# Three edits ahead of a matmul-bound stage: which queue issues loads, where weight roundings are doubled, and when weight sums begin

## The chip, the cores and the metric

The kernel runs on one core of a Trainium2 chip. The metric is the device time of one execution in microseconds, the median of three executions. PE is TensorE, DVE is VectorE, ACT is ScalarE, POOL is GpSimd and SP is SyncE. SP computes nothing here; it only issues DMAs. Every engine works through its own instructions in order.

## What is computed

Two blocks follow each other. The first is an attention with a threshold, for 8 batches of 8 heads, 576 rows and 64 values per head:

```python
scores = scale * np.matmul(q, k.transpose(0, 1, 3, 2))
thresh = np.max(scores, axis=-1, keepdims=True) - tau
scores = np.where(scores >= thresh, scores, -1000000000.0)
attn = np.exp(scores - max); attn = attn / (sum + 1e-09)
attn_out = np.matmul(attn, v)
```

(The last three lines are shortened.) The heads are put side by side, which gives `x`, 4608 rows of 512 values, and the second block follows:

```python
h = x @ w_in
r = np.maximum(h, 0.0)
g = r * r
return (g @ w_out).astype(np.float32)
```

`w_in` is 512 x 2048 and `w_out` is 2048 x 512, all in float32.

## The kernel before

**Steps.** Attention is cut into visits and steps. A visit `n` is a pair of heads of a batch (in the first batch, visits 0 to 3 take blocks 0 and 1 of it and visits 4 to 7 the rest); a step `s` is one block `i` of 128 query rows of a visit, for both heads. Block 4 is the leftover of 64 rows; the leftovers of the two heads, or from visit 12 on of two visits, share one step. There are 148 steps, and the main loop (L758 to L849) writes out the order of the work by hand, step after step. The trace has no step numbers; one counts the bursts of score matmuls on PE (L250), each of which starts a step.

**One step.** `scores` (L241) runs the score matmuls into PSUM and takes the row maxima on DVE (L272). `exponents` (L282) makes a bias and a threshold from the maxima and the exponents of both heads on ACT (L285, L286, L288). `threshold` (L291) applies the mask on DVE, one instruction per head (L300), and computes the reciprocals of the sums. `divide` (L305) scales the rows on POOL (L308, L310). A score tile of PSUM is free for the next step when its mask is done.

**Turning the weights of attention.** Up to visit 10, two steps later, PE transposes the rows (`turn`, L325) and ACT copies them to `wT`; three steps later `mix` (L433) multiplies with `v` (L436), and ACT puts the result into `xT`. From visit 11 on (`by_dma`, L602; its first step is 35, named `first_dma`), DVE transposes 32 x 32 squares (`turn_blocks`, L351, instruction L374) and SP places them with DMAs (`place_blocks`, L377, lines L386 to L399, 16 per call); visit 11's three placings come in steps 38, 39 and 40, and its `mix` in step 43.

**Loads.** `load_qk` (L160) issues the `q` and `k` rows of a visit on SP, except that for a `by_dma` visit it appends them with `load_part` (L177) to the list `loads`. `some_loads` (L191) is called four times a step; each call takes one or two entries from the front of that list and issues them on POOL (L194). Visit 11 is the one `by_dma` visit that goes through `load_qk` (step 31), and its `v` rows (`load_v`, L199, called at the end of step 34) go out on POOL too (L213). Later visits append directly, by the lists made at L708 to L741: in step 36 the `k` rows of visit 12, in step 37 those of visit 13 and the `q` rows of visit 12. `prep_part` (L227) transposes loaded rows on DVE (L230) into `qT` and `kT`. At the last step of a visit before `by_dma` (there `lay` is true, L786), `prep` does so for the next visit between the maxima and the masks. In the second step of such a visit, `split_left` (L220) copies the leftover query rows to `qmid` on ACT (L225).

**Roundings.** The weights arrive in 32 pieces, by DMAs on SP (L125), into three areas. Each piece is put into another form in five stages (`round_weights`, L127): two ACT instructions (stage 0, L138 and L139), one on DVE (stage 1, L141), one on DVE (stage 2, L143), two on POOL (stage 3, L145, and stage 4, L147). When it is done (`end_rounding`, L701), the area's next load is issued. The list `pieces` (L689 to L696) says how many pieces each step rounds. In a step with one, stage 1 stands between the exponents and the masks, stages 2 and 3 after the masks (in a `lay` step stage 1 too is after the masks). A second piece of a step (L824) has stages 1 to 3 after the masks. Steps with two are 16, 19 and 24, each of them a leftover step.

**Filling PE.** The matmuls of the second block are cut into filling pieces of eight matmuls (in the count of the trace): `mlp_in` (L477, matmuls L484), for the first chunk of 256 rows `mlp_out` (L511, L520), and for later chunks `product` (L539, L553). `fill` (L676) is called four times a step and puts pieces between the work of attention as far as the budget of the step allows (`rate`, L651) and as far as the weights they need were rounded by the step before last (`usable`). So a piece of weights that is rounded in an earlier step lets filling pieces move to an earlier step. The ACT and POOL work on their results is posted after the next piece.

**Weight sums.** The products of later chunks need sums of quarters of `w_out`, made by `some_sums` (L504) in 16 parts, one DVE instruction each (L508). They write where the areas of the arriving weights were (the first six parts) and beyond. A part is posted after each `mlp_in` piece of chunk 1 once `state["free"]` is set (L812), from the middle of step 36 on; `product` asks for those that it needs.

Of the kernel before, what the change touches and what calls it, by code (L numbers as in the profile page):

```python
# [19 lines left out]
def kernel(  # L20
# [10 lines left out]
    nc = tc.nc  # L31
# [4 lines left out]
    HP = H // 2  # L36
    NPAIR = B * HP
    NBLK = S // P
    REST = S - NBLK * P
# [66 lines left out]
    n_pieces = n_in + NFT * d_model // WP  # L106
# [43 lines left out]
    def rows_of(n):  # L150
        return rows_in[n % 2 if n <= 2 * HP else 0]
# [3 lines left out]
    def rows_32(t, n, m):  # L155

        b, h = divmod(visits[n][0], HP)
        return t[b, 2 * h + m // 2, :, (m % 2) * 32:(m % 2) * 32 + 32].rearrange("(c p) d -> p c d", p=32)

    def load_qk(n):  # L160


        if by_dma(n):
            load_part(k, n)
            load_part(q, n)
            return
        for x, t in ((rows_of(n)[1], k), (rows_of(n)[0], q)):
            for m in range(4):
                src, to = rows_32(t, n, m), x[m * 32:(m + 1) * 32, :, :]
                queue = nc.scalar if n == 0 and m % 2 else nc.sync  # L170
                last = REST // 32 if t is k and m >= 2 else 0
                queue.dma_start(out=to[:, last:, :], in_=src[:, 0:S // 32 - last, :])
                if last:
                    queue = nc.gpsimd if n == 0 else nc.sync
                    queue.dma_start(out=to[:, 0:last, :], in_=src[:, S // 32 - last:, :])

    def load_part(t, n):  # L177
        x = rows_of(n)[0 if t is q else 1]
        loads.extend((x[m * 32:(m + 1) * 32, :, :], rows_32(t, n, m)) for m in range(4))
# [11 lines left out]
    def some_loads():  # L191
        for _ in range(min(1 + (len(loads) > 8), len(loads))):
            to, src = loads.popleft()
            nc.gpsimd.dma_start(out=to, in_=src)  # L194

    def arrived(t):
        assert all(x[0].tensor.name != t.tensor.name for x in loads)
# [1 line left out]
    def load_v(n):  # L199
        b, h = divmod(visits[n][0], HP)  # L200
        h *= 2
        t = vs[n % 2]
        todo = []
        for u in range(2):
            at = u * (NBLK + 1)
            todo.append((t[:, at:at + NBLK, :], v[b, h + u, 0:NBLK * P, :].rearrange("(c p) d -> p c d", p=P)))
            for half in range(2):
                todo.append((t[half * D:(half + 1) * D, at + NBLK, :], v[b, h + u, NBLK * P:S, :]))
        if paired(n):
            loads.extend(todo)  # L210
            return
        for to, src in todo:
            (nc.gpsimd if by_dma(n) else nc.sync).dma_start(out=to, in_=src)  # L213

    def prep(n):

# [260 lines left out]
    def mlp_in(j, x):  # L477

        f, at = FORDER[x], j * TCH % RING
        if x % 2 == 0:  # L480
            used["h"] = take("mm", (6, 7)) if j < PLAIN else next_bank()
        h = used["h"].rearrange("p (f n) -> p f n", f=2)
        for c in range(NMC):
            nc.tensor.matmul(h[:, x % 2, :], w_in_sb[:, c, f * P:(f + 1) * P], xT[:, c, at:at + TCH],  # L484
                             start=(c == 0), stop=(c == NMC - 1))
        if x == NFT - 1:
            read_to["x"] = (j + 1) * TCH
        posts = []
        if j == PLAIN and state["free"]:
            posts.append(lambda: some_sums(1))  # L490
        if x % 2:
            def square():
                to = g[:, f - 1:f + 1, :]
                nc.scalar.activation(out=to, in_=h, func=AF.Relu)  # L494
                nc.gpsimd.tensor_tensor(out=to, in0=to, in1=to, op=ALU.mult)  # L495
                if j >= PLAIN and x % 8 == 7:
                    square_half(x // 8 * (HF // 2))
            posts.append(square)
        return posts

    sums = [(to, a, b, part) for to, a, b in ((FT1, Q01, Q00), (FT2, Q11, FT1), (FT4, FT2, Q10), (FT3, Q11, Q01))
            for part in range(4)]

    def some_sums(count):  # L504

        for to, a, b, part in sums[:count]:
            f = slice(part * 2, part * 2 + 2)
            nc.vector.tensor_tensor(out=wo[:, to, f, :], in0=wo[:, a, f, :], in1=wo[:, b, f, :], op=ALU.subtract)  # L508
        del sums[:count]
# [77 lines left out]
    FIRST = TCH // P  # L587
# [3 lines left out]
    def paired(n):  # L591

        return n >= 3 * HP
# [6 lines left out]
    PLAIN = 1  # L600

    def by_dma(n):  # L602

        return n >= 3 * HP - 1

    first_dma = next(s for s in range(NST) if by_dma(steps[s][0]))
# [19 lines left out]
    chunk_at, j = {}, 0  # L626
# [7 lines left out]
    state = {"us": 0.0, "left": 0.0, "step": 0, "free": False, "rounded": 0, "usable": 0, "then": [], "last": []}  # L634
# [55 lines left out]
    for s, (n, i) in enumerate(steps):  # L690
        if s < HP * FIRST:
            x = int(n > 0 and i == 0)
        else:
            x = 2 if HP + 2 <= n <= 2 * HP and i == NBLK else 1
        pieces.append(min(x, left))
        left -= pieces[-1]  # L696
    assert left == 0
# [58 lines left out]
    done = 0  # L756
    rounded_by = [0]
    for s in range(END + 1):  # L758
        state["step"] = s
        state["usable"] = rounded_by[-1]  # L760
        if s == 2:
            startup.close()
            bpsum = ctx.enter_context(tc.tile_pool(name="bpsum", bufs=1, space=bass.MemoryType.PSUM))
            bank.update((x, bpsum.tile([P, 512], FP32, tag=f"bank{x}", name=f"bank{x}")) for x in range(4, 8))
        rounded_by.append(state["rounded"])
        on = s < NST
        now = []
        if on:
            n, i = steps[s]
            at = visits[n][1].index(i)  # L770
            last = at == len(visits[n][1]) - 1
            now = list(range(done, done + pieces[s]))
            done += pieces[s]
            more = n + 1 < len(visits)
            short = n < 2 * HP
            if short and at == 0 and 0 < n + 1 < 2 * HP:
                load_qk(n + 2)
            elif not short and at == 1 and not by_dma(n):
                load_qk(n + 1)
            if now:  # L780
                round_weights(now[0], 0)
            if s != 1:
                scores(s)
        old = steps[s - 2] if 2 <= s < NST + 2 and not by_dma(steps[s - 2][0]) else None
        at_once = now or old or early()
        lay = on and last and more and not by_dma(n)  # L786
        if old:
            turn(*old, 0)
            turn(*old, 1)
        if on:  # L790
            exponents(n, i)
            for p in now[1:]:
                round_weights(p, 0)
            if at == 1:
                split_left(n)
            if lay:
                prep(n + 1)
            elif now:
                round_weights(now[0], 1)
        if s in mixes and not old:  # L800
            mix(*mixes[s])
            for j in chunk_at.get(s, ()):
                add_chunk(j)
        quarter = rate(s) / 4 if s < END else 1e9
        fill(quarter)
        if s in mixes and old:
            mix(*mixes[s])
            for j in chunk_at.get(s, ()):
                add_chunk(j)
        if old:  # L810
            turn(*old, 2)
        state["free"] = s > first_dma  # L812
        if s == 0:
            scores(1)
        if on:
            threshold(n, i)
            for fn in prep_at[s] + load_at[s]:
                fn()
            if lay and now:
                round_weights(now[0], 1)  # L820
            if now:
                round_weights(now[0], 2)
                round_weights(now[0], 3)
            for p in now[1:]:  # L824
                for stage in range(1, 4):
                    round_weights(p, stage)
            if not at_once:
                divide(n, i)
        if 0 < s <= NST and by_dma(steps[s - 1][0]):
            m, x = steps[s - 1]  # L830
            turn_blocks(m, x)
        for what in place_at[s]:
            place_blocks(*what)
        some_loads()
        fill(quarter)
        some_loads()
        if on and at_once:
            divide(n, i)
        fill(quarter)
        some_loads()  # L840
        fill(quarter)
        some_loads()
        if on:
            for p in now:
                end_rounding(p)
            if at == 0 and 0 < n <= 2 * HP:
                load_v(n)
            elif last and n >= 2 * HP and not by_dma(n):
                load_v(n + 1)  # L849
# [35 lines left out]
```

## Time and profile before

| | before |
|---|---|
| executions | 1394.46, 1396.89, 1398.92 us |
| profiled execution | 1396.9 us, span of the instructions 1395.1 us |
| PE, DVE, ACT, POOL busy | 97%, 60%, 31%, 65% of the span |
| PE busy in 0-100, 100-200, 200-300 us | 83.25, 94.79, 91.09 us |
| PE busy in 300-400 us | 100.00 us |
| granted PE clock, mean | 0.993 |
| SP DMAs that place (L386 to L399) | 1008 |

Busy time is the time in which an engine runs at least one instruction; issuing and waiting are not counted, except that the loads issued by POOL show up as POOL instructions (L194, L213). A row of a list of groups or of the timeline gives engine, line, operation, what is written from what (tile names without numbers), and a count; in square brackets stands the idle time before it and what ended it. `w`, and `wo` where L300 or L310 write it, are the tiles of attention rows: one of the three slots lies in the memory of `wo`. `turned` is scratch for roundings and, later, for the squares that are placed.

### The profile page before, as it was taken

Reading aid. Unit: us, or ns where it says so; the run is one execution under the profiler, and the core shown is the slowest. Engines: PE = TensorE matmul, PEld = TensorE weight load, DVE = VectorE, ACT = ScalarE, POOL = GpSimd, SP = SyncE. Lnnn points to the kernel's source line nnn. Section 1 sums busy time; section 2 is a strip of 40 time slices with the busy share of each in tenths; the row PEclk is TensorE's granted clock in tenths of the full one; section 3 lists DMA queues with packets and bytes.
Section 4 is the critical chain, followed back from the end, with each engine's and each line's share of the span. In section 5 each row is a group of like instructions: output and inputs, shape, how many; then the busy total and the mean of one; then the engine's idle time right before and its main releaser. Section 6 shows DMA issues by size and latency. Waiting matters only on the chain.

```text
span 1395.1 us, 22691 instructions
## 1 busy us (share of the span) xinstructions
PE 1356.8 (97%) x7576; PEld 1042.1 (75%) x7576; DVE 830.8 (60%) x1866; ACT 439.5 (31%) x1068; POOL 909.7 (65%) x1233
## 2 busy tenths in 40 slices
PE   6898998999999999999999999999999999999998
PEld 5676556777777778777777778777777877788887
DVE  5877774976767676757575666566666665401001
ACT  4776673223232323232323222222222222210110
POOL 3688877678696868676767677685867655422332
PEclk8999999999999999999999999999999999999999
DMA  8764521435646555554445455544444544310000
GB/s 153 156 146 135 135 64 40 78 80 110 118 95 110 112 104 116 99 115 85 98 84 115 82 111 109 109 79 101 90 99 89 121 87 101 63 35 16 0 16 16
DMA packets 397892, 127.95 MB, mean 92 GB/s; under 512 B 380336, under 2 KB 386576, under 8 KB 397776
## 3 DMA queue, kind: packets, MB, share of 16 engines
q1 hardware_dynamic: 374496, 93.07, 35.4%
q0 software_dynamic: 20976, 33.14, 8.9%
q8 instruction: 61, 1.00, 0.3%
q10 hardware_dynamic: 2304, 0.29, 0.2%
q14 instruction: 55, 0.45, 0.1%
HBM read 50.59 MB, written 9.44 MB: 43 GB/s over the span
## 4 chain that ended last, share of the span: by engine, by line
PE 89%; DVE 4%; ACT 2%; issue 2%; POOL 2%; DMA 1%; POOLq 0%; DVEq 0%; SPq 0%; ACTq 0%
PE bank L484 35%; PE bank L553 28%; PE s L250 12%; PE bank L436 10%; PE bank L520 2%; PE bank L334 2%; DVE wo L508 1%; DVE w L300 1%; ACT w L288 1%; DVE st L272 1%; ACT wT L335 1%; POOL kl L194 0%; POOL w L310 0%; DVE turned L374 0%; DVE wo L300 0%
## 5 line engine op out<-in xcount | busy, mean ns | idle before, releaser
L484 PE MATMUL bank<-xT,w_in_sb 128*128 128x256 f32 x2304 | 520.8, 383 | 1.1 <-ACT osb L526 1.1
L484 PEld LDWEIGHTS bank<-xT,w_in_sb 128*128 128x128 f32 x2304 | 432.2, 190 | 82.9 <-issue 22.2
L272 DVE TENSOR_REDUCE st<-s 128x1 f32<-128x576 f32 x286 | 203.9, 752 | 231.2 <-PE s L250 231.2
L300 DVE SCALAR_TENSOR_TENSOR w<-s,st,w 128x576 f32<-128x576 f32 x269 | 209.2, 814 | 119.4 <-ACT w L288 119.1
L553 PE MATMUL bank<-wo,gsum 128*128 128x256 f32 x1088 | 248.9, 382 | 2.1 <-POOL gsum L474 2.0
L310 POOL TENSOR_SCALAR w<-w,st 128x576 f32<-128x576 f32 x269 | 220.5, 829 | 25.2 <-DVE st L303 19.3
L553 PEld LDWEIGHTS bank<-wo,gsum 128*128 128x128 f32 x1088 | 204.0, 190 | 41.2 <-issue 9.8
L495 POOL TENSOR_TENSOR g<-g 128x512 f32<-128x512 f32 x144 | 151.3, 1051 | 97.6 <-ACT g L494 96.2
L285 ACT ACTIVATE st<-st 128x2 f32<-128x2 f32 (+1 forms) x148 | 30.3, 205 | 571.4 <-DVE st L272 570.6
L553 PE MATMUL bank<-wo,g 128*128 128x256 f32 x816 | 188.3, 382 | 0.0
L250 PE MATMUL s<-kT,qT 64*128 64x288 f32 x1016 | 168.2, 435 | 19.4 <-DVE w L300 6.9
L288 ACT ACTIVATE w<-s,st 128x576 f32<-128x576 f32 x269 | 183.1, 731 | 0.2 <-ACT st L286 0.2
L374 DVE STREAM_TRANSPOSE turned<-w 128x512 f32<-128x512 f32 (+2 forms) x388 | 168.8, 489 | 18.1 <-DMA wT<-turned 16.3
L308 POOL TENSOR_SCALAR st<-st 128x2 f32<-128x2 f32 (+1 forms) x148 | 33.4, 225 | 221.9 <-DVE w L300 214.7
L553 PEld LDWEIGHTS bank<-wo,g 128*128 128x128 f32 x816 | 153.0, 190 | 30.0 <-issue 8.3
L436 PE MATMUL bank<-wT,vs 128*64 128x128 f32 (+7 forms) x1700 | 167.9, 356 | 3.9 <-ACT wT L335 3.5
L436 PEld LDWEIGHTS bank<-wT,vs 128*64 128x64 f32 (+1 forms) x1700 | 95.7, 136 | 77.0 <-issue 23.8
L250 PEld LDWEIGHTS s<-kT,qT 64*128 64x128 f32 x1016 | 95.4, 189 | 76.6 <-issue 56.5
L494 ACT ACTIVATE g<-bank 128x512 f32<-128x512 f32 x144 | 86.0, 599 | 196.0 <-PE bank L484 195.3
L194 POOL DMA_DIRECT2D vs<-in_v_dram x144 | 90.5, 634 | 0.0
L567 DVE TENSOR_TENSOR gsum<-g 128x512 f32<-128x512 f32 x34 | 23.2, 714 | 110.6 <-PE bank L553 110.6
L194 POOL DMA_DIRECT2D kl<-in_k_dram x100 | 68.6, 689 | 0.0
(81 smaller groups left out, 997.4 us busy)
## 6 DMA issues: line engine op xcount, KB each, us to landing
wT<-turned SPq DMA_DIRECT2D x800, 72.0 KB, 2.3
out_dram<-osb POOLq DMA_DIRECT2D x34, 256.0 KB, 2.7
wo<-in_moe_w_in_dram SPq DMA_DIRECT2D x16, 512.0 KB, 4.7
wo<-in_moe_w_out_dram SPq DMA_DIRECT2D x16, 512.0 KB, 3.6
kl<-in_k_dram POOLq DMA_DIRECT2D x100, 72.0 KB, 3.0
ql<-in_q_dram POOLq DMA_DIRECT2D x100, 72.0 KB, 2.7
wT<-turned SPq DMA_DIRECT2D x192, 36.0 KB, 2.4
vs<-in_v_dram POOLq DMA_DIRECT2D x50, 128.0 KB, 3.2
```

The lines of the kernel that those rows point to most:

```text
L194: nc.gpsimd.dma_start(out=to, in_=src)
L250: nc.tensor.matmul(sc[u][to, half, 0:HALF], lhsT, keys[rows, half * HALF:(half + 1) * HALF], start=True, stop=True)
L272: nc.vector.tensor_reduce(out=mx[:, u:u + 1], in_=sc[u][:, :, 0:HALF], axis=AX.XY, op=ALU.max)
L288: nc.scalar.activation(out=w[:, u, :].rearrange("p (h k) -> p h k", h=2), in_=sc[u][:, :, 0:HALF], func=AF.Exp, bias=bias[:, u:u + 1], sca ...
L300: nc.vector.scalar_tensor_tensor(out=wu, in0=sc[u][:, :, 0:HALF], scalar=thr[:, u:u + 1], in1=wu, op0=ALU.is_ge, op1=ALU.mult, accum_out=s ...
L310: nc.gpsimd.tensor_scalar(out=w[:, u, :], in0=w[:, u, :], scalar1=z[:, u:u + 1], scalar2=rcp[:, u:u + 1], op0=ALU.add, op1=ALU.mult)
L374: nc.vector.transpose(wb[:, at:at + k1 - k0, i % 2, :], w[:, u, k0 * 32:k1 * 32].rearrange("p (k q) -> p k q", q=32))
L436: nc.tensor.matmul(ps[u * D:(u + 1) * D, :], vs[n % 2][rows, u * (NBLK + 1) + c, :], wT[rows, NBLK if c == NBLK else u * (NBLK + 1) + c, a ...
L484: nc.tensor.matmul(h[:, x % 2, :], w_in_sb[:, c, f * P:(f + 1) * P], xT[:, c, at:at + TCH], start=(c == 0), stop=(c == NMC - 1))
L494: nc.scalar.activation(out=to, in_=h, func=AF.Relu)
L495: nc.gpsimd.tensor_tensor(out=to, in0=to, in1=to, op=ALU.mult)
L553: nc.tensor.matmul(to, left[:, f, :], wo[:, slot, f, :], start=(f == 0), stop=(f == HF - 1))
```

## The change

There are three edits.

- Loads: `load_qk` no longer appends the loads of a `by_dma` visit to the list, but issues them at once on SP; `load_v` issues on SP where it issued on POOL; `some_loads` issues on SP up to step 37 and on POOL after that. This touches the eight `q` and `k` loads of visit 11, its six `v` loads, and the eight `k` loads of steps 36 and 37.
- Roundings: the steps with two pieces are 15, 18 and 22 instead of 16, 19 and 24. In such a step stage 1 of both pieces stands ahead of the masks; stages 2 and 3 of both follow after them. The order of the filling pieces on PE follows from what is `usable`: steps 15 to 28 hold 1,1,2,1,1,2,1,2,1,2,1,1,2,1 of them, where they held 1,1,0,2,2,0,3,1,1,2,1,2,1,2.
- Sums: the first parts may be made before `state["free"]`, up to six of them, as soon as all weight pieces are rounded. Parts per step, from 35 on: 2,4,4,3,3,0 where they were 0,2,4,3,5,2.

```diff
@@ load_qk
-        if by_dma(n):
-            load_part(k, n)
-            load_part(q, n)
-            return
         for x, t in ((rows_of(n)[1], k), (rows_of(n)[0], q)):
...
-                last = REST // 32 if t is k and m >= 2 else 0
+                last = REST // 32 if t is k and m >= 2 and not by_dma(n) else 0
@@ some_loads
-            nc.gpsimd.dma_start(out=to, in_=src)
+            (nc.gpsimd if state["step"] > first_dma + 2 else nc.sync).dma_start(out=to, in_=src)
@@ load_v
-            (nc.gpsimd if by_dma(n) else nc.sync).dma_start(out=to, in_=src)
+            nc.sync.dma_start(out=to, in_=src)
@@ mlp_in
-        if j == PLAIN and state["free"]:
+        if j == PLAIN:
             posts.append(lambda: some_sums(1))
@@ some_sums
+        done = 16 - len(sums)
+        count = min(count, (16 if state["free"] else 6 if state["rounded"] == n_pieces else 0) - done)
         for to, a, b, part in sums[:count]:
@@ pieces
-            x = 2 if HP + 2 <= n <= 2 * HP and i == NBLK else 1
+            x = 2 if (n, i) in ((2 * HP - 2, FIRST + 1), (2 * HP - 1, FIRST + 1), (2 * HP, FIRST)) else 1
@@ main loop, before the masks
             elif now:
-                round_weights(now[0], 1)
+                for p in now:
+                    round_weights(p, 1)
@@ main loop, after the masks
             for p in now[1:]:
-                for stage in range(1, 4):
-                    round_weights(p, stage)
+                assert not lay
+                round_weights(p, 2)
+                round_weights(p, 3)
```

## Prediction

> **What bounds the kernel now.** I read the table of windows first, because shares of the whole span hide stages. Columns: window and length; busy time of PE, PEld, DVE, ACT, POOL, each with its count; granted clock; DMA share; GB/s.
>
> ```profile
> 100.00:120.00 20.00, 17.08 (x130) 12.89 (x131) 15.13 (x30) 13.11 (x33) 17.97 (x21) 0.91 0.45 125
> ...
> 200.00:220.00 20.00, 16.16 (x124) 10.30 (x123) 12.40 (x33) 11.18 (x27) 18.63 (x24) 1.00 0.13 30
> ...
> 260.00:280.00 20.00, 16.79 (x85) 13.02 (x85) 18.71 (x35) 4.19 (x11) 12.97 (x17) 1.00 0.43 80
> ...
> 300.00:400.00 100.00, 100.00 (x539) 76.05 (x536) 68.49 (x161) 30.55 (x76) 74.22 (x107) 1.00 0.58 113
> ```
>
> From about 280 us PE is busy without a break: there its work alone sets the time, and the edit doesn't change that work. Holes lie at 100-120 (clock at 0.91), 200-220 (POOL nearly full) and 260-280 (DVE nearly full), the stages that the edit touches. So its worth is the PE idle time it removes before 280 us. Next, who PE waits for; the list of waits gives total, times, longest. The first line is of 84-165 us, the others of 190-300 us.
>
> ```profile
> PE s L250 <- DVE w L300: 2.9, 2, 2.3
> ...
> PE s L250 <- DVE wo L300: 2.6, 1, 2.6
> PE s L250 <- DVE qT L230: 2.6, 1, 2.6
> PE bank L484 <- ACT osb L526: 1.1, 1, 1.1
> PE bank L520 <- POOL wo L147: 0.9, 1, 0.9
> ```
>
> The first ends at 109.92, the 2.6 before `wo` at 218.70, the 2.6 on `qT` at 279.80; a wait of 0.8 before step 39 is left out here. The chain of waits and the timeline show their causes.
>
> ```profile
> 103.45 1.26 issue
> 104.72 0.42 DVE turned L141
> ...
> 106.46 1.42 DVE st L272 x2
> ...
> 112.30 3.36 PE bank L484 x8
> ```
>
> Two roundings (L141, L143) run back to back on DVE in step 16 and hold the row maxima of step 17 until 106.46, though its scores began at 103.04. PE idles; then eight matmuls take 3.36 us instead of 1.73.
>
> ```profile
> 213.06 1.38 POOL L194 DMA_DIRECT2D ql<-in_q_dram  x2
> ...
> 216.40 0.78 DVE L230 STREAM_TRANSPOSE qT<-ql 128x576 f32<-128x576 f32 x1 [2.39 <-DMA ql<-in_q_dram]
> ...
> 269.82 4.65 DVE L508 TENSOR_TENSOR wo<-wo 128x512 f32<-128x512 f32 x4
> ```
>
> The last `q` loads of visit 11 are issued by POOL only at 213.06, between its other work; DVE waits 2.39 us for them. In step 39, four weight sums delay the maxima of step 40 to 274.40 and so `qT` to 278.87.
>
> **What the Trainium skill says.** "SBUF — State Buffer", section Who interferes with whom: VectorE in a two-port mode, or with two SBUF inputs against a GpSimd op that reads SBUF, and GpSimd exclude each other for a whole instruction. The trace agrees: L143 takes 0.41 us with POOL idle and 1.38 us at 103.42 beside a POOL add; an L508 takes 0.68 us alone and 4.65/4 = 1.16 us here. "DMA: Bandwidth & Descriptors", section SWDGE vs HWDGE vs iDMA: descriptors of DMAs issued from GpSimd are written by its own cores, those of SyncE by hardware. The trace agrees that POOL pays: eight L194 at 200-220 us are 5.68 us busy, 0.71 each. "TensorE: Matmul & The Clock Gate", section Part 1: idle windows of about 3.4 us halve the clock. The trace shows the 0.91 and the doubled matmuls after the 2.3 us hole, but 2.6 us holes at 218 and 280 that did not trigger it; so it is a risk, not a rule.
>
> **The change, part by part.** Steps are the code's; I number the bursts of L250. One filling piece (eight matmuls) is 1.73 us.
>
> *Loads.* Eight `k`/`q` loads of visit 11 (steps 31, 32), six `v` loads (step 34) and eight `k` loads (steps 36, 37) leave POOL for SP. POOL loses 5.7 + 3.7 (L213, six) + 8 x 0.7 = 15 us before 260 us. SP issues a load in 2.05/4 = 0.51 us; its last wait ahead is the weight load of step 30, so visit 11's land by about 207. Step 33: the wait for POOL L147 (0.94) goes. Step 34: now maxima end at 214.0, transposes could end at 215.5, the mask at 216.3, against 218.55; that is 2.3 us. SP's `k` loads of step 37 wait for DVE's `kT` at 249.3 and put 4 x 0.5 us in front of the placing that began at 250.84: 0.5 us late at most, hidden, as SP idles from 261.6 to 270.05. The `v` loads and step 36's loads cost nothing on the path: SP is empty there, and the transposes that need them had no DMA wait. Sum: **-3.3 us** (bounds -2 to -4).
>
> *Sums.* Four of sixteen L508 leave steps 39-40 for steps 35-36. There DVE is busy only 16.68 of 33.21 us, so they cost nothing. Step 39 keeps two of its four after the transposes: 4.65/2 = 2.3 us off the maxima of step 40, hence off `qT`. The two of step 40 lay in the shadow of ACT's exponents and behind `qT`: nothing. PE's own work in step 40 (16 score matmuls 1.77 + four pieces 6.9) ends at 276.6, `qT` would end at 277.4, so DVE still decides: **-2.3 us**. The 0.8 us wait before step 39 stays, the same three sums being ahead of it. The placing of visit 11 restarts at 270.05, 32 issues of 0.67 to 291.5, landing 2.3 later, 293.8; its consumer moves from 297.5 to 295.2. It still fits, by 1.4 us. Bounds 0 to -3.5.
>
> *Roundings.* Doubles move from steps 16, 19, 24 (one head pair's leftover, with the two `q`,`k` transposes) to 15, 18, 22. Each carries two ACT, two DVE, two POOL instructions and one weight load on SP; the load waits for the ACT reads, and the `v`/`q`/`k` loads behind it have two steps of slack. New wait: the second L141, now ahead of the masks, needs ACT's L138, which stands behind both exponents. In step 15 exponents end at 96.96, L138 at about 97.65, L141 at 98.06: masks start at 98.06, not 96.37, **1.7 us later**. Queued behind it are the masks; scores of the next step wait for them, and the `qmid` copies wait behind 1.26 us more on ACT. After the masks come two L143, the second shut out by POOL's multiplication of the first (1.3 us). Step 16's maxima then come at about 102.0 instead of 99.04, scores 17 at 105.2 instead of 103.04. But the masks of step 17 need no more to wait for four roundings, and PE has pieces meanwhile: with both weights ready a step sooner, the filling becomes 1,1,2,1,1,2,1 pieces in steps 15-21 instead of 1,1,0,2,2,0,3. Step 17 is then PE-bound (5.6 with one piece, 7.3 with two, from steps 25 and 28) and ends at 112.5 with two pieces more than before had at 109.92: 0.9 us ahead. The half-clock stretch (3.36 - 1.73 = 1.6 us) goes. At 18 and 19, the mask cost returns: 125.1 against 125.45. Steps 20-21 end 1.6 us ahead at the same count; step 22 has two pieces, hiding the third late mask. At step 29 I get **-2.0 us**. The trace of before doesn't show two L141 ahead of the masks; bounds: +4 (three late masks and shut-outs bare, 3 x 3.0, less the old wait and half clock, 2.3 + 0.5 + 1.6) to -4 (no cost; 4.4 all gained).
>
> Sum: -3.3 - 2.3 - 2.0 = -7.6. The profiled execution took 1396.9 us (span 1395.1); the others were 1394.46 and 1398.92, so it is the median. Forecast: 1396.9 - 7.6 = **1389.3 us**.
>
> **Rivals.**
> - *Roundings give nothing.* For: the DVE work between 93 and 106 us is the same, in another order, and a wait is added. Against: PE has a spare hole there. Then -3.3 - 2.3: 1391.3; with +1.5 lost, 1392.8.
> - *Everything opens.* The half clock and all old waits of 84-165 vanish (-4.4), POOL's freedom also shortens the sums of step 37 and the 0.8 wait (-3.1), loads -4: 1385.4. Against: the POOL ops that shut out those sums are L474/L475, which stay.
> - *Placing becomes the bound.* SP starts later or DMA is slower by over 1.4 us; PE waits at the first placed mix, and the sums' gain is lost: 1391.6.
> - *Slower: late masks with half clock.* Each of steps 15, 18, 22 leaves PE a hole of 1.7 + 1.3 us that also halves the clock (1.6): 3 x 4.6 = 13.8, less 4.4 of old costs and 5.6 of the other parts: +3.8, 1400.7. For: the 2.3 us hole did halve it once. Against: one or two pieces per step fill the hole. It decides from 3.3 us per site, (5.6 + 4.4)/3.
> - *Loads bring nothing,* another wait replacing the `ql` one: 1392.6. Against: nothing else in step 34 ends after 215.5.
>
> **How the numbers follow.** Forecast 0.50 (1387 to 1391.5); roundings nothing 0.20; everything opens 0.12; placing 0.06; loads nothing 0.05; slower 0.05; no effect at all 0.02. A measurement tells about 0.3%, 4.2 us, from no change: below 1392.7 is faster. That takes the forecast, the opening, placing and some half of the roundings and loads cases: 0.79; within: 0.16; slower: 0.05. The range 1384.5 to 1395.0 takes in both bounds of the loads and sums, and roundings from -4 to +3.5 at the middle of the others; it leaves out the slow rival and the far ends.
>
> **What would show it.** Loads: no DMA wait before L230 in step 34, step 35 starting some 3 us earlier against step 31, no L194 on POOL before step 38. Sums: L508 in step 35, and at most 0.9 us of idle PE before step 41. Roundings: clock 1.00 in 100-120, masks of 15, 18, 22 starting 1.7 us later after their scores, no PE wait above 1.5 us before L250 in 90-165. After step 43 the spans should be equal within 1 us; a difference there would make my frame wrong, as would a new wait of L436 for the placing.

## The result, and the profile after

| | before | after |
|---|---|---|
| median | 1397.88 us (4 runs, 1394.46 to 1398.92) | 1389.95 us (4 runs, 1389.86 to 1391.53) |
| ratio | | 0.995, 95% interval 0.9931 to 0.997 |
| span of the profiled execution | 1395.1 us | 1389.8 us |

The change is faster by about 0.5% (0.3% to 0.7%). Lines of the kernel after are 4 lower from `load_qk` on (scores L246, maxima L268, mask L296, filling matmul L480), 1 lower from L507 on (the sums were L508). First the table of windows, with the columns of before.

```profile
100.00:120.00 20.00, 17.06 (x140) 12.47 (x139) 15.35 (x29) 13.60 (x36) 17.59 (x18) 1.00 0.40 118
200.00:220.00 20.00, 19.43 (x144) 12.52 (x143) 14.37 (x37) 14.04 (x37) 15.42 (x18) 1.00 0.17 32
260.00:280.00 20.00, 19.02 (x96) 14.74 (x96) 18.26 (x34) 5.85 (x15) 14.29 (x18) 1.00 0.52 97
300.00:400.00 100.00, 100.00 (x529) 77.05 (x529) 67.65 (x156) 29.97 (x74) 76.23 (x109) 1.00 0.59 117
```

The holes at 200-220 and 260-280 are filled (PE 16.16 to 19.43 and 16.79 to 19.02). That at 100-120 is not: PE is busy for 17.06 us where it was 17.08, though the clock is full now. PE's waits, of 190-300 us:

```profile
PE bank L480 <- ACT osb L525: 1.1, 1, 1.1
PE s L246 <- DVE qT L226: 0.4, 1, 0.4
PE s L246 <- DVE wo L296: 0.3, 1, 0.3
```

The 2.6 us on `wo` and the 2.6 us on `qT` are down to 0.3 and 0.4. Of 84-165 us:

```profile
PE bank L480 <- POOL w_in_sb L147: 2.1, 4, 0.5
...
PE s L246 <- DVE w L296: 1.2, 1, 1.2
```

The old wait of 2.3 us for the mask is gone, and a new one stands first: filling matmuls that wait for weights that POOL writes last (L147). The chain of waits of after, from 104 us:

```profile
104.33 1.17 PE s L246 x8
105.50 0.82 PE bank L330 x6
...
106.36 2.50 POOL w_in_sb L147 x2
...
108.91 0.70 PE bank L480 x2
```

In step 17 the end of the step hangs on two roundings' last additions on POOL.

Counting bursts of score matmuls gives each step's length, and so where the 5.36 us between the profiles come from (start of step 15 to the end, in us):

| steps | before | after | difference |
|---|---|---|---|
| 15 to 28 (roundings) | 90.94 | 91.72 | +0.78 |
| of these, 17 and 20 | 6.88, 4.75 | 8.87, 8.91 | |
| 29 to 34 | 35.17 | 31.64 | -3.53 |
| 35 to 37 | 33.21 | 33.21 | 0 |
| 38, 39 | 7.41, 8.61 | 6.70, 8.43 | -0.89 |
| 40 | 11.86 | 9.80 | -2.06 |
| 41 to the end | 1115.32 | 1115.56 | +0.24 |

(+0.10 lies ahead of step 15.) The medians differ by 7.9 us, the profiled executions by 5.4 (1396.89 and 1391.53). Of the 2.6 us between, 1.0 lies with the kernel before: its profiled execution is that much below its median. It holds one window of half clock in these stages, and other executions hold more, as the experiments show. The other 1.6 lies with the kernel after: its profiled execution is the slowest of its four, and the others took 1389.86 to 1389.96. It reaches step 15 at 92.69 us (before at 92.59), where nine of the eleven profiles of the experiments below reach it at 90.07 to 91.35. The three other executions of after have no profile, so where they gained their 1.6 us is not shown.

### The profile page after: what moved, and what is told of

It is laid out like the page before. It is cut to its first block, busy times and chain, and to the rows that moved or that the text cites. A ratio compares the mean times of both kernels' runs of the same rounds, so it can differ in the third digit from the quotient of the medians.

```text
span 1389.8 us, 22678 instructions
## 1 busy us (share of the span) xinstructions
PE 1354.5 (97%) x7576; PEld 1039.6 (75%) x7576; DVE 828.9 (60%) x1866; ACT 439.8 (32%) x1068; POOL 899.3 (65%) x1211
## 3 DMA queue, kind: packets, MB, share of 16 engines
q0 software_dynamic: 19984, 31.63, 8.4%
## 4 chain that ended last, share of the span: by engine, by line
PE 89%; DVE 3%; ACT 3%; POOL 2%; issue 1%; DMA 1%; SPq 0%; DVEq 0%; ACTq 0%; POOLq 0%
PE bank L480 34%; PE bank L552 29%; PE s L246 12%; PE bank L432 11%; PE bank L519 2%; PE bank L330 2%; ACT wT L331 1%; ACT w L284 1%; DVE wo L507 1%; DVE w L296 1%; DVE st L268 1%; POOL g L491 0%; POOL w L306 0%; POOL w_in_sb L147 0%; DVE wo L296 0%
## 5 line engine op out<-in xcount | busy, mean ns | idle before, releaser
L480 PE MATMUL bank<-xT,w_in_sb 128*128 128x256 f32 x2304 | 520.4, 382 | 3.2 <-POOL w_in_sb L147 2.1
L480 PEld LDWEIGHTS bank<-xT,w_in_sb 128*128 128x128 f32 x2304 | 430.8, 190 | 85.8 <-issue 22.2
L268 DVE TENSOR_REDUCE st<-s 128x1 f32<-128x576 f32 x286 | 204.1, 753 | 224.4 <-PE s L246 224.3
L296 DVE SCALAR_TENSOR_TENSOR w<-s,st,w 128x576 f32<-128x576 f32 x269 | 209.2, 815 | 120.6 <-ACT w L284 120.5
L306 POOL TENSOR_SCALAR w<-w,st 128x576 f32<-128x576 f32 x269 | 223.5, 840 | 25.2 <-DVE st L299 19.2
L246 PE MATMUL s<-kT,qT 64*128 64x288 f32 x1016 | 166.9, 435 | 12.1 <-DVE kT L226 4.9
L246 PEld LDWEIGHTS s<-kT,qT 64*128 64x128 f32 x1016 | 94.9, 189 | 69.1 <-issue 49.0
L145 POOL TENSOR_TENSOR turned<-turned 128x512 f32<-128x512 f32 x32 | 41.1, 1288 | 40.7 <-DVE turned L143 34.9
```

The lines of the kernel that those rows point to most:

```text
L246: nc.tensor.matmul(sc[u][to, half, 0:HALF], lhsT, keys[rows, half * HALF:(half + 1) * HALF], start=True, stop=True)
L268: nc.vector.tensor_reduce(out=mx[:, u:u + 1], in_=sc[u][:, :, 0:HALF], axis=AX.XY, op=ALU.max)
L296: nc.vector.scalar_tensor_tensor(out=wu, in0=sc[u][:, :, 0:HALF], scalar=thr[:, u:u + 1], in1=wu, op0=ALU.is_ge, op1=ALU.mult, accum_out=s ...
L306: nc.gpsimd.tensor_scalar(out=w[:, u, :], in0=w[:, u, :], scalar1=z[:, u:u + 1], scalar2=rcp[:, u:u + 1], op0=ALU.add, op1=ALU.mult)
```

## The experiments

Each experiment takes the kernel before or after and does or undoes a part. Steps 15 to 28 are given as a sum. Steps 17 and 20 are given too: in the new order they come two steps after doubled roundings and hold two filling pieces each. Every step length is of one profiled execution.

**Alone, or left out.** The three edits of the diff are separable. The first of these runs has the loads and sums hunks without the two roundings hunks; the others have one edit each, all on the kernel before.

> The loads and sums edits without the roundings edit. In the trace of the changed kernel steps 15 to 28 take 91.7 us, 0.8 more than before's 90.9, and steps 29 to 40 take 6.5 us less. Theory 'the roundings cost': this kernel keeps before's 90.9 and gains the 6.5, so it is about 0.8 us faster than the changed kernel, some 7 us (0.50 to 0.55%) under before, and the half clock near 112 us comes back. Rival 'the roundings gain 2 us, as predicted, and the two profiles compared were unlike': it is 2 us slower than the changed kernel, some 5 us under before.

> The roundings edit alone. Theory 'the roundings cost': steps 15 to 28 take 91.7 us instead of 90.9; 0 to 1 us slower than before in all. ACT waits some 4 us for POOL's last stage (L147) in steps 17 and 20, and no half clock. Rival 'as predicted': steps 15 to 28 take 88.9, 2 us faster than before.

> The loads edit alone. If the parts add up: steps 29 to 34 take 3.5 us less than before's 35.2, and step 37 or 38 some 0.7 us less, because the sums of step 37 no longer stand behind POOL's load issues: 3.5 to 4.2 us under before (0.25 to 0.30%). Rival 'the 0.7 us of step 38 belong to the sums edit': 3.5 and no change in step 38.

> The sums edit alone. If the parts add up: step 40 takes 2.1 us less than before's 11.9 and nothing else moves: 2.1 to 2.3 us under before (0.15%). Rival 'the 0.7 us of step 38 belong to the sums edit': 2.8 to 3.0 us, with step 38 at 6.7 instead of 7.4 us.

| | median, us | ratio to before, interval | steps 15-28 | 29-34 | 38 | 40 |
|---|---|---|---|---|---|---|
| loads and sums | 1389.16 | 0.994, 0.9924 to 0.9957 | 92.20 | 31.64 | 6.69 | 9.79 |
| roundings | 1399.07 | 1.0001, 0.9992 to 1.0011 | 91.70 | 35.21 | 7.41 | 11.86 |
| loads | 1393.27 | 0.9963, 0.9951 to 0.9975 | 92.24 | 31.64 | 6.69 | 12.07 |
| sums | 1393.65 | 0.9972, 0.9961 to 0.9984 | 90.96 | 35.11 | 7.40 | 9.58 |

The kernel before had 1398.94 us beside them. Loads and sums together bring all that the change brings; the roundings edit alone brings nothing that can be measured. In steps, loads are worth 3.5 in 29-34 and 0.7 in 38, and the rival that gave this 0.7 to the sums is out. With loads alone step 40 takes 0.2 us more than before (12.07 against 11.86); so the sums are worth 2.3 us in step 40 both without the loads (11.86 to 9.58) and beside them (12.07 to 9.79).

The medians fell by more than these steps add up to: by 5.7 us with the loads, by 5.3 with the sums, by 9.8 with both. Fewer windows of half clock can be the rest, as the next paragraphs show, but how much of it they are was not measured.

The old roundings' sums 90.94 and 92.2 are one program: the two runs of 92.2 show half clock for 6.8 us, from 108.5 to 115.4 us (step 18 takes 10.23 and 10.28 us), the others for 3.4 us (8.99 and 9.01). The clock halves there in all six profiles with the old roundings and in none of the seven with the new. The roundings-alone run shows half clock elsewhere, although none at all was expected of it. Windows of that run around its two later holes:

```profile
216.00:226.00 10.00, 7.78 (x21) 4.54 (x22) 5.70 (x14) 3.17 (x8) 8.27 (x13) 0.66 0.11 34
280.00:288.00 8.00, 5.58 (x21) 4.18 (x22) 7.92 (x17) 1.99 (x7) 5.37 (x8) 0.79 0.60 115
```

The clock is 0.66 and 0.79 behind the waits for `wo` and `qT` (2.7 and 2.6 us here) which in the profile before left it at 1.00. Step 35 takes 16.89 us instead of 13.79, step 41 9.92 instead of 8.28. So the same hole costs 1.6 or 3.1 us more in one execution and nothing in another. Over the 22 runs of this kernel the span goes with the mean clock: 1394.1 to 1394.6 us at 0.995 or 0.996, 1394.2 to 1397.1 at 0.994, 1397.5 to 1399.4 at 0.991 or 0.992. The four runs of the changed kernel all stand at 0.994 or 0.995. This fits the 1.0 us by which the profile before lies below its median; it doesn't explain the 1.6 us of after.

**Which load.** Only the `load_qk` hunks of the diff (the `q` and `k` loads of visit 11).

> Of the loads edit only the eight q and k loads of visit 11 go to SP; the v loads and those of steps 36 and 37 stay on POOL. Theory: steps 33 and 34 take 5.66 and 4.30 us as with the whole loads edit (6.87 and 6.62 before), step 38 stays at before's 7.41, so the 0.7 us there come from the loads of steps 36 and 37. Rival 'the v loads of step 34 do it': step 38 at 6.69 here or step 35 changed.

One run, 1392.1 us. Steps 29-34 take 31.63 us: the whole gain there is from these eight loads, and the six `v` loads bring nothing. Step 38 stays at 7.41, so its 0.7 belongs to the others. POOL and DVE rows of this run's timeline:

```profile
245.21 0.70 POOL L190 DMA_DIRECT2D kl<-in_k_dram  x1
245.56 5.33 DVE L504 TENSOR_TENSOR wo<-wo 128x512 f32<-128x512 f32 x3
...
245.93 1.05 POOL L491 TENSOR_TENSOR g<-g 128x512 f32<-128x512 f32 x1
...
247.06 1.61 POOL L470 TENSOR_TENSOR gsum<-g 128x512 f32<-128x512 f32 x1
248.74 1.59 POOL L471 TENSOR_TENSOR gsum<-gsum,g 128x512 f32<-128x512 f32 x1
```

And of the kernel after, three sums again:

```profile
247.62 1.05 POOL L491 TENSOR_TENSOR g<-g 128x512 f32<-128x512 f32 x1
247.95 4.62 DVE L507 TENSOR_TENSOR wo<-wo 128x512 f32<-128x512 f32 x3
248.75 1.59 POOL L470 TENSOR_TENSOR gsum<-g 128x512 f32<-128x512 f32 x1
...
250.42 1.60 POOL L471 TENSOR_TENSOR gsum<-gsum,g 128x512 f32<-128x512 f32 x1
```

With one load issue (0.70 us) in front, POOL's three instructions begin after the sums do, and each of the three sums meets one of them: 5.33 us. Without it the first is already running, and the sums take 4.62. Taken singly they are 1.98, 1.75 and 1.75 us with the load issue, and 1.27, 1.75 and 1.75 without it: the whole 0.71 us lies in the first sum. This places the gain of step 38 with the `v` loads or the `k` loads of steps 36 and 37; the row of 245.21 is one of the latter.

**Is it the scratch?** In the kernel after, ACT waits 8.0 us, in two waits, in 82-165 us for POOL's L147 before it may write stage 0 of a later piece, since `turned` has three slots of scratch. The first run adds a fourth slot to the kernel after, the second to the kernel with loads and sums only.

```diff
-        t, e, d = (turned[:, (i % 3 * 3 + x) * WP:(i % 3 * 3 + x + 1) * WP] for x in range(3))
+        if i % 4 == 3:
+            spot = gsum[0].rearrange("p f n -> p (f n)"), gsum[1].rearrange("p f n -> p (f n)")
+            t, e, d = spot[0][:, 0:WP], spot[0][:, WP:2 * WP], spot[1][:, 0:WP]
+        else:
+            t, e, d = (turned[:, (i % 4 * 3 + x) * WP:(i % 4 * 3 + x + 1) * WP] for x in range(3))
```

> The changed kernel with four scratch areas for the roundings instead of three (the fourth lies in gsum, which is idle then). Theory 'the doubled roundings run out of scratch': in steps 17 and 20 ACT no longer waits 4 us for POOL's last stage of the piece three before, so steps 17 and 20 fall from 8.87 and 8.91 us to 7.3 to 8.0; about 2 to 3 us faster than the changed kernel, 0.7% under before. Rival 'it is PE waiting for the weights of its filling pieces': PE's waits on L147 (2.1 us) stay, steps 17 and 20 stay above 8.5, the time is that of the changed kernel. Rival 'late masks': steps 15 and 18 (6.34, 6.66) are the whole loss and don't change here either.

> Loads and sums edits, the roundings as before, four scratch areas. In before, ACT waits 1.2 us for POOL in step 17 and DVE stands behind it. Theory 'the hole of step 17 is DVE's back to back roundings and its shut-outs': the hole and the half clock of step 18 stay, the time is that of the kernel without the roundings edit (0.6% under before). Rival 'scratch is the cause there too': step 17 falls from 6.9 to 6 us or less, no half clock, 2 us or more faster than that kernel.

The first took 1388.62 us (ratio to before 0.9933, 0.9921 to 0.9946), the second 1389.39 (0.9937, 0.9925 to 0.995). With the fourth slot in the kernel after, ACT's list of waits in 82-165 us is headed by this row, and no other of its rows names POOL:

```profile
ACT wT L335 <- PE bank L334: 12.6, 11, 3.4
```

PE's list of the same run and window is headed by this one (L484 and L151 are L480 and L147 of after):

```profile
PE bank L484 <- POOL w_in_sb L151: 2.4, 4, 0.7
```

ACT no longer waits for POOL at all, and yet PE still does: steps 17 and 20 take 9.08 and 9.03 us, 15-28 together 91.31. The scratch falls as the cause of these two steps. It was a long wait off the path. Only step 24 gets shorter by more than 0.4 us (7.33 where it took 7.91). With the old roundings the slot gains nothing (91.15, with a half-clock window as before had it).

**The masks.** The kernel after with the doubled steps where it has them, but stages 1 to 3 of the second piece behind the masks, as the main loop before has it.

```diff
             elif now:
-                for p in now:
-                    round_weights(p, 1)
+                round_weights(now[0], 1)
...
             for p in now[1:]:
-                assert not lay
-                round_weights(p, 2)
-                round_weights(p, 3)
+                for stage in range(1, 4):
+                    round_weights(p, stage)
```

> The changed kernel with all three DVE stages of the second rounding behind the masks. Theory 'late masks cost 1.1 us in step 15 and 1.3 in step 18 where PE has nothing to fill': step 15 is back at 5.28 and step 18 at 5.3 to 5.7, step 22 no shorter; steps 17 and 20 as in the changed kernel; 1 to 2 us faster than it. Rival 'the DVE work is only put off': steps 16 and 19 grow by what 15 and 18 lose, the time is that of the changed kernel.

1387.28 us (1385.71 to 1388.62; ratio to before 0.9921, 0.9907 to 0.9935). Steps 15 and 18 shrink by 0.40 and 0.71 us, steps 16 and 19 grow by 0.42 and 0.44. But steps 17 and 20 fall to 7.78 and 7.77, which neither expectation had, and steps 15-28 to 88.78: 2.9 us less than after, 2.2 less than before. So the edit has two halves of opposite sign: moving the doubled steps gains 2.2 us against a profile that holds 3.4 us of half clock, stage 1 ahead of the masks costs 2.9, of which 2.2 lie in steps 17 and 20. The late masks themselves cost nothing in steps 15 and 16: in after the second mask of step 15 starts at 98.80, here at 97.23, both steps 15 begin at 92.69, and yet both steps 17 begin at 104.26 and 104.28. In step 18 they do cost something: the 1.2 us for which PE waits in after for a mask (L296, in the list above) end at the start of step 19. The cost in step 17 comes at POOL. Its rows in the timeline of after, with DVE's row of the two L143 ahead of them:

```profile
99.93 0.74 DVE L143 TENSOR_SCALAR turned<-turned 128x512 uint32<-128x512 uint32 x2
...
100.48 2.56 POOL L145 TENSOR_TENSOR turned<-turned 128x512 f32<-128x512 f32 x2 [4.20 <-DVE turned L143]
103.12 0.22 POOL L304 TENSOR_SCALAR st<-st 128x2 f32<-128x2 f32 x1
103.44 1.79 POOL L306 TENSOR_SCALAR w<-w,st 128x576 f32<-128x576 f32 x2
105.20 1.20 POOL L491 TENSOR_TENSOR g<-g 128x512 f32<-128x512 f32 x1
106.36 2.49 POOL L147 TENSOR_TENSOR w_in_sb<-turned 128x512 f32<-128x512 f32 x2
```

POOL sits idle for 4.20 us until the first piece's L143, which the later masks have pushed back, and then works without a gap: stage 3 of both, the scaling, the multiplication of `g`, stage 4 of both. Only then do the pieces of step 17 have their weights. With stage 1 of the second piece behind the masks POOL starts at 98.90 and L147 at 105.09:

```profile
98.90 1.33 POOL L145 TENSOR_TENSOR turned<-turned 128x512 f32<-128x512 f32 x1 [2.62 <-ACT xT L415]
...
105.09 2.69 POOL L147 TENSOR_TENSOR w_in_sb<-turned 128x512 f32<-128x512 f32 x2
```

**POOL's order.** If this chain is the cause, a new order on POOL alone must shorten steps 17 and 20. Stage 4 of doubled steps is put ahead of the multiplication of `g`:

```diff
         if on and at_once:
             divide(n, i)
+            if len(now) > 1:
+                for p in now:
+                    end_rounding(p)
...
-            for p in now:
+            for p in now * (len(now) == 1):
                 end_rounding(p)
```

The first run has it on the kernel of the last experiment, the second on the kernel after; the third is as the first, but with stage 4 of the first piece ahead of `divide` too.

> The second rounding's stages behind the masks again, and in the doubled steps the two last additions on POOL (they write the weights) stand right behind the scaling of the attention weights, ahead of the multiplication of g. Theory (POOL's order sets when the filling pieces of steps 17 and 20 get their weights): these steps were 7.78 and 7.77 us with the stages behind the masks; they fall to PE's own 7.3, so steps 15 to 28 take about 87.8 us, and the time is about 1386.4. Rival (the exponents and masks set these steps): 7.8 each, 88.8, 1387.3.

> The changed kernel with only that move of POOL's two last additions. Theory: the multiplication of g (1.20 us) no longer stands ahead of them, so steps 17 and 20 fall from 8.87 and 8.91 us to about 7.7 each, steps 15 to 28 from 91.7 to about 89.4, and the time to about 1387.6. Rival (the late masks hold the exponents and the scores, POOL only looks like the cause): steps 17 and 20 stay at 8.9, time 1389.9.

> As the first of this call, but the first of the two additions stands ahead of the scaling of the attention weights. Theory: the weights come 2 us sooner still, which PE can't use any more, and the scaling comes 1.25 us later, which holds the turning of the attention weights that follows the next scores: steps 17 and 20 take 7.3 to 8.0, time 1386.4 to 1387.8. Rival (POOL's order doesn't matter): as with the stages behind the masks, 1387.3.

| | median, us | ratio to before, interval | steps 17, 20 | 15-28 |
|---|---|---|---|---|
| on the last experiment's kernel | 1385.94 | 0.9919, 0.9903 to 0.9935 | 7.30, 7.30 | 87.73 |
| on the kernel after | 1388.17 | 0.9933, 0.9916 to 0.9949 | 7.86, 7.91 | 89.99 |
| with the first ahead of `divide` | 1385.62 | 0.9915, 0.9897 to 0.9932 | 7.30, 7.37 | 87.81 |

The theory holds: only POOL's order was touched, and on the kernel after both steps lose 1.0 us (and step 24, two steps after the third doubled step, 0.6), on the other kernel they reach 7.30, the length that step 28 of before (7.28) has with two filling pieces. The later scaling of the third run, which was to cost something, shows at most in step 20 (7.37), and the run came out below the 1386.4 to 1387.8 that was expected. POOL in the first of the three:

```profile
100.56 1.62 POOL L306 TENSOR_SCALAR w<-w,st 128x576 f32<-128x576 f32 x2
102.15 2.85 POOL L147 TENSOR_TENSOR w_in_sb<-turned 128x512 f32<-128x512 f32 x2
104.97 1.04 POOL L491 TENSOR_TENSOR g<-g 128x512 f32<-128x512 f32 x1
```

L147 stands right behind L306, and PE has no wait for it left. On the kernel after the gain was less than forecast (15-28 at 89.99, not 89.4), mainly because the stage 1 ahead of the masks now costs more in step 18. DVE and PE of that run, in step 18:

```profile
115.55 1.58 DVE L141 TENSOR_SCALAR turned<-turned 128x512 uint32<-128x512 uint32 x1 [1.74 <-ACT turned L138]
...
117.05 0.80 DVE L296 SCALAR_TENSOR_TENSOR w<-s,st,w 128x576 f32<-128x576 f32 x1
...
118.00 0.97 PE L246 MATMUL s<-kT,qmid 128*128 128x288 f32 x3 [2.06 <-ACT turned L138]
```

The masks wait behind the second L141, which waits for ACT, and PE waits 2.06 us; step 18 takes 7.49 us where it took 6.66. In after, where step 17 is a microsecond longer, this wait is 1.2 us. The first and the third version are the fastest of the study, some 4 us below the changed kernel in the time and in steps 15-28 (87.73 and 87.81 against 91.72), though the intervals of the ratios to before overlap by a hair; a difference between the two isn't resolved.

## Why the prediction was right, and where it was not

The time, 1389.95 us against 1389.3, and its sign and range were right, but in part by luck. The forecast took 7.6 us off the profiled execution of before. The two profiled executions differ by 5.4, so the terms as they came out give 2.2 us less than the forecast, the roundings above all. The time agrees because the median of after lies 1.6 us below its profiled execution, of which the prediction says nothing. Term by term:

- **Loads, -3.3: right, and 0.7 more.** Steps 29-34 gave 3.53, from `q` and `k` of visit 11 alone. The `v` loads cost and brought nothing, as said. The rival that another wait takes their place is out. Not in the sum were steps 38 and 39, -0.89, and the 0.2 by which step 40 grows with loads alone. Most of this is step 38: the sums of step 37 start when POOL's multiplication is already under way, once no load issue stands ahead of it. The text had named this under "everything opens" and set it aside because L474 and L475 stay; they stay, but start earlier.
- **Sums, -2.3: right.** Step 40 loses 2.28 us alone and as much beside the loads; the change as a whole shows 2.06, the 0.2 of the loads being in it. PE waits 0.4 us before step 41, under the 0.9 said. Two sums run between 216 and 232 us at 0.68 us each. The placing still fits: no `mix` waits for it, and steps 42 to 48 have the lengths of before. The sentence that the 0.8 us before step 39 stays was wrong; the loads took most of it.
- **Roundings, -2.0: wrong.** They gave +0.78 against the profiled execution and no difference in 22 runs alone; the rival that they give nothing had 0.20. Two steps of its working failed. "With both weights ready a step sooner" took what the program may use for what is there: `usable` counts steps of the program, but POOL wrote those weights at 106.36 to 108.85, inside the step that uses them. "Step 17 is then PE-bound" followed, 7.3 us, where 8.87 were measured; it ended at 113.13, not 112.5, although it began at 104.26, 0.9 ahead of the 105.2 said. The second step that failed was smaller: the two L143 were not shut out (1.3 us), but ran in 0.74 us, POOL's L145 beginning only towards their end (100.48). The masks did start at 98.06, as said (though step 15 began 0.10 us later than in before), and cost nothing there. The half-clock stretch near 112 us did go.
- **Half clock: a risk, as said, but it was priced too small.** It was counted at one window, 1.6 us. The holes at 218 and 280 can trigger it too (1.6 or 3.1 us in the roundings-alone profile), and the change takes away both; near 112 us the clock stays full too. This can be the 1.0 us by which the median of before lies above its profiled execution; it enters the 7.9 us between the medians, but not the forecast of the time, which started from the profile.
- **The slow rival,** three late masks with half clock each, did not come: the clock is 1.00 in 100-120 and no wait of PE before L246 is above 1.2 us in 84-165.
- **The frame held:** after step 43 the profiles differ by 0.24 us.
- **Two slips in the working:** the upper bound of the roundings is 9.0 less 4.4, which is 4.6 and not 4; and step 25, read as 5.6 us with one filling piece, takes 5.87. The forecast rests on neither.

What would be better is shown too: the doubled steps of the change, the second stage 1 behind the masks, and stage 4 ahead of the multiplication of `g`, 1385.9 us.

## What to carry to other kernels

When work is moved a step earlier so that another engine may use its result, follow that result to the last instruction that writes it, on its own engine's queue, and compare that time with the first use; a counter in the program that allows the use is not the time of the result. An instruction that is put ahead on one queue delays not only what stands right behind it, but the queue of the next engine too, and the bill may come two steps later. The longest wait in the list need not be the one on the path: take it away alone, and see whether the step gets shorter.

## What was not expected of the hardware

The hole of PE of 2.6 to 2.7 us before step 35 halves the clock in one of the three profiles that have it, the like hole before step 41 in two of four; the hole of 2.3 us (2.7 in one) in step 17 of before does so in all six profiles that have it. The half clock lasts about 3.4 or 6.8 us and costs 1.6 or 3.1 us in steps 41 and 35. The Trainium skill ("TensorE: Matmul & The Clock Gate", Part 1) speaks of idle windows of about 3.4 us; the windows seen here have that length and its double (four times it at the start of the program), but the holes ahead of them are shorter.

The stretches of half clock lie on a grid. By the granted clock in each of the 13 profiles, all of them begin a whole number of times 3.413 us apart: in the roundings-alone profile at 13.02, 23.26, 217.82 and 282.67 us, that is 0, 3, 60 and 79 periods after the first. Where the grid lies in the program differs from one execution to the next, and with it how a hole is cut up. The first row below is the grid period of the roundings-alone profile that ends where the half clock begins; the other two are the periods over which the same hole falls in the profile before, where the clock stayed full.

```profile
214.41:217.82 3.41, 1.13 (x13) 0.55 (x9) 1.89 (x3) 1.20 (x3) 3.22 (x5) 1.00 0.09 22
...
214.15:217.56 3.41, 1.90 (x23) 1.31 (x23) 1.16 (x2) 1.97 (x6) 3.20 (x5) 1.00 0.17 43
217.56:220.97 3.41, 2.27 (x15) 1.68 (x16) 2.34 (x7) 0.52 (x2) 3.22 (x5) 1.00 0.00 0
```

PE is busy for 1.13 us of the one, for 1.90 and 2.27 us of the two. Before step 41 it is alike: 0.77 us in one period of the roundings-alone profile, 1.56 and 2.61 us in two of before. So a hole seems to count when most of it falls into one period. It isn't the whole rule: near 110 us of before two neighbouring periods with 2.11 and 1.81 us of PE work were enough, and where the limit lies is not shown.

The lock between DVE and POOL depends on who starts first by tenths of a microsecond: three sums took 4.62 or 5.33 us beside the same POOL additions and multiplication, by whether one 0.70 us load issue stood ahead of those.
